# A first strip of 576 tokens, batch 1 normalised by token, and another order of loads, in a fused attention and bilinear feed-forward kernel

## The chip, the cores and the metric

One core of a Trainium2 chip runs the whole program. The metric is the device time in microseconds (us) of one execution; the time before is the median of three runs. The profile is one further execution of the same program, read engine by engine: PE is the matrix engine, PEld its weight loads, DVE the vector engine, ACT the scalar engine, POOL the GpSimd engine, SP the sync engine, which here issues stores and transposing DMAs.

## The reference

```python
kv  = einsum('bhsd,bhse->bhde', k, v)            # per batch b and head h, 64 x 64
x   = einsum('bhsd,bhde->bhse', q, kv)
x   = x / sqrt(mean(x * x, -1) + 1e-6) * g_norm  # RMS norm over the 64 of a head
x   = x.transpose(0, 2, 1, 3).reshape(4608, 512) # tokens by features
out = (x @ w_a) * (x @ w_b) @ w_out              # 512 -> 1536 -> 512
```

There are 8 batches of 576 tokens and 8 heads of 64. All inputs and the output are float32; the kernel multiplies in bfloat16 and accumulates in float32.

## The kernel before

The feed-forward part is cut into 9 strips of 512 tokens. `xt` holds x in bfloat16 with features on partitions, 4 blocks of 128. For a strip s, `ffn_ab(s, fc)` (line 389) computes one of 12 chunks of 128 hidden features: 4 matmuls with `wa_t` into one PSUM bank, a copy of it to SBUF by ACT (`part_a`), 4 matmuls with `wb_t` into another bank, and the product of both by DVE into `abt` (`part_b`). Then `ffn_o(s, g)` (line 434) computes the output of 128 tokens, g = 0 to 3, by 12 matmuls; `o_out` copies the bank to SBUF, on DVE when its running number is even and on ACT when it is odd, and `store` sends it out by SP in two pieces or so.

x comes from the attention of a batch, which is worked in between the matmuls of a strip. Strips do not end with batches: strip 2 is tokens 1024 to 1535, and batch 2 is tokens 1152 to 1727.

- Batch 0, at the start, and batch 1, between the output pieces of strip 0 (the loop over `pieces`, line 575), go **by feature**. For each of 4 pairs of heads: `qtr` transposes q on PE (12 matmuls), `kv1` makes k'v (12 matmuls), `x` or `px` multiplies, `psq` squares on ACT, `pss` sums the squares with a matmul against `ones` and takes the root on ACT, and `pst` scales on DVE straight into `xt`.
- Batches 2 to 7 go **by token**, in `slot(A, s, n)` (line 601), which is called after unit n of strip s, and with n - 0.5 in the middle of unit n. Units 0 to 11 are the chunks, 12 to 15 the output groups. `kv` makes k'v at `k0`; at `x0` `tx` makes x with tokens on partitions in 40 small matmuls, for 5 chunks c of 128 tokens (the last of 64). For each c then `tsq` squares (ACT), `tss` sums (DVE), `trs` takes the root (ACT) and multiplies it with g (POOL), and `txt` multiplies x with that (DVE) and has SP transpose the chunk into `xt` with a DMA.

Each engine runs its instructions in the order in which the code emits them, so the emission order is the schedule. POOL issues the loads and SP the stores and the transposing DMAs, each in that order too. Every POOL or SP DMA also waits for the one eight before it on its queue, whose semaphore it reuses.

`load_late(b)` (line 136) issues six DMAs on POOL for a batch from 2 on: two that rewrite q by token in bfloat16 into the DRAM tensor `qs`, and four that load k and v. For b > 2 it first has POOL copy one element of `qT[(b-1) % 2]`, so that it waits for the q of the batch before. `transpose_q(b)` (line 153) has SP transpose `qs` into `qT`. At the start POOL issues batch 0, then w_a and w_b in six chunks of 256 hidden features, then w_out in 12 pieces, batch 1 in 12 pieces, and `load_late(2)`.

`halves[0]` makes `product` issue two matmuls with 64 weight columns each in place of one with 128; such a pair runs side by side.

Of the kernel before, what the change touches and what calls it, by code (L numbers as in the profile page):

```python
# [15 lines left out]
def kernel(  # L16
# [11 lines left out]
    nc = tc.nc  # L28
# [14 lines left out]
    EARLY = 2  # L43
    KORD = tuple(range(KC))

    pool = ctx.enter_context(tc.tile_pool(name="sb", bufs=1))
    psum = ctx.enter_context(tc.tile_pool(name="ps", bufs=1, space=bass.MemoryType.PSUM))

# [17 lines left out]

    qT = [sb([128, NP, S], BF16, f"qT{i}") for i in range(2)]
    kvs = [sb([128, NP, D], BF16, f"kvs{i}") for i in range(2)]

    kvb = sb([128, NP, 128], BF16, "kvb")  # L70
    xt = sb([128, KC, n_tok], BF16, "xt")
    abt = [[sb([128, STRIP], BF16, f"ab{i}_{f}") for f in range(FC)] for i in range(2)]
    a_sb = [sb([128, STRIP], BF16, f"asb{i}") for i in range(4)]
    sq = [sb([128, 2, HF], BF16, f"sq{i}") for i in range(3)]
    rs = [sb([128, 2, HF], FP32, f"rs{i}") for i in range(3)]
# [58 lines left out]
        nc.gpsimd.dma_start(out=wo_t[:, i, :], in_=wo_v[:, i, :])  # L134

    def load_late(b):
        if b > EARLY:

            nc.gpsimd.tensor_copy(gate, qT[(b - 1) % 2][0:1, 0, 0:1])  # L139
        d = qs_d[b].rearrange("t (h d) -> t h d", h=H)  # L140
        for hs in (slice(0, NP), slice(NP, H)):
            nc.gpsimd.dma_start(out=d[:, hs, :], in_=q[b, hs].rearrange("h t d -> t h d"))  # L142
        n = 128 * LC
        for t, src in ((ktl[b % 2], k), (vtl[b % 2], v)):
            nc.gpsimd.dma_start(  # L145
                out=t[:, :, 0:LC, :],
                in_=src[b, :, 0:n].rearrange("h (t c) d -> t h c d", c=LC),
            )
            nc.gpsimd.dma_start(
                out=t[0 : S - n, :, LC, :], in_=src[b, :, n:].rearrange("h t d -> t h d")  # L150
            )
# [12 lines left out]
    class Attn:  # L164
# [5 lines left out]
        def kv(self, p, o):  # L170
# [5 lines left out]
            for c, n in enumerate(rows):  # L176
                for j in range(2):
# [4 lines left out]
                        start=(c == 0),  # L182
                        stop=(c == len(rows) - 1),
                    )

        def kv_out(self, ps, src):
            for j in range(2):
                r = slice(j * D, (j + 1) * D)
                nc.scalar.copy(kvb[r, ps, r], src[r])


        def kv1(self, p, i):
# [57 lines left out]
                )  # L250


        def x(self, p, i0):
            for h in range(2):
                product(
                    P[:, i0 + h, 0:HF],
                    kvb[:, p, :],
                    self.qT[:, p, h * HF : (h + 1) * HF],
                    start=True,
                    stop=True,  # L260
                )

        def rows(self, c):
            t0 = min(c * 128, S - 128)
# [19 lines left out]
        def tx(self, lent):  # L286
            self.lent = lent
            for c in range(LC + 1):
                t0, _ = self.rows(c)
                for p in range(NP):  # L290
                    for j, (i, c0) in enumerate(self.place(c)):
                        r = slice(j * D, (j + 1) * D)
                        nc.tensor.matmul(  # L293
                            P[:, i, c0 + p * D : c0 + (p + 1) * D],
                            lhsT=self.qT[r, p, t0 : t0 + 128],
                            rhs=self.kvs[r, p, :],
                            start=True,
                            stop=True,
                        )


            _, r = self.rows(LC)
            for j, (i, _) in enumerate(self.place(LC)):
                nc.scalar.copy(
                    x_last[r, j], P[r, i, 0 : STRIP // 2].rearrange("t (p d) -> t p d", p=NP)
                )

        def tsq(self, c):
            _, r = self.rows(c)
# [7 lines left out]
                axis=mybir.AxisListType.X,  # L317
            )

        def trs(self, c):  # L320
            _, r = self.rows(c)
            n = r.stop - r.start
            nc.scalar.activation(  # L323
                rst[c % 3][r],
                sst[c % 3][r],
                AF.Abs_reciprocal_sqrt,
                bias=eps_t[r],
                scale=1.0 / D,
            )
            nc.gpsimd.tensor_mul(  # L330
                sqt[c % 3][r].rearrange("t j p d -> t (j p) d"),
                rst[c % 3][r].unsqueeze(2).to_broadcast([n, H, D]),
                g_all[r].unsqueeze(1).to_broadcast([n, H, D]),
            )
# [13 lines left out]
    class Unit:  # L348
        n = 0

        def __init__(self, s, fc, a, b):
            self.s, self.fc, self.a, self.b = s, fc, P[:, a, :], P[:, b, :]
            self.t = a_sb[Unit.n % 4]
            Unit.n += 1

        def mm(self, w, kcs):
            t0 = self.s * STRIP
            for kc in kcs:
                product(
                    self.a if w is wa_t else self.b,  # L360
                    w[:, kc, self.fc * 128 : (self.fc + 1) * 128],
                    xt[:, kc, t0 : t0 + STRIP],
                    start=(kc == KORD[0]),
                    stop=(kc == KORD[-1]),
                )
# [2 lines left out]
            self.mm(wa_t, kcs)  # L368
            self.mm(wb_t, kcs)

        def part_a(self, kcs=KORD):
            self.mm(wa_t, kcs)
            nc.scalar.copy(self.t, self.a)  # L373

        def part_b(self, kcs=KORD):
            self.mm(wb_t, kcs)
            nc.vector.tensor_mul(abt[self.s % 2][self.fc], self.b, self.t)  # L377

        def rest(self, kcs=KORD):
            self.part_a(kcs)  # L380
            self.part_b(kcs)

    ab_banks = [4, 1, 2, 0]

# [4 lines left out]
    def ffn_ab(s, fc, between=None):  # L389
        u = Unit(s, fc, ab_bank(), 0)  # L390
        u.part_a()
        if between:
            between()
        u.b = P[:, ab_bank(), :]
        u.part_b()

    def store(t0, t, e0, e1, eng=nc.sync):
# [14 lines left out]
    n_o = [0]  # L412

    def o_mm(s, g, i, fcs, e0=0, e1=d_model):
        for fc in fcs:
            product(
                P[:, i, e0:e1],
                abt[s % 2][fc][:, g * 128 : (g + 1) * 128],
                wo_t[:, fc, e0:e1],
                start=(fc == 0),  # L420
                stop=(fc == FC - 1),
# [42 lines left out]
    make_identity(nc, ident, nomemset=True)  # L464
    nc.scalar.activation(warm, eps_t, AF.Abs_reciprocal_sqrt)
    nc.vector.memset(ones, 0.0)
    nc.vector.memset(kvb, 0.0)
    for t in ktl + vtl:
        nc.vector.memset(t[S - 128 * LC :, :, LC, :], 0.0)
    nc.vector.memset(ones[0:D, 0:D], 1.0 / D)  # L470
# [4 lines left out]
    for c in range(0, KC, 2):  # L475
        for w, src in ((wa_t, wa_v), (wb_t, wb_v)):
            nc.gpsimd.dma_start(out=w[:, c : c + 2, 0:WC], in_=src[:, c : c + 2, 0:WC])  # L477
    for i in range(1, d_ff // WC):
        load_ab(i * WC, (i + 1) * WC)
    for i in range(FC):  # L480
        load_o(i)
    for p in range(NP):
        load_pair(1, p)
    load_late(2)

    X, SS = (4, 0), 6

# [65 lines left out]
    u1.part_a((3,))  # L553
    u0.part_b((2, 3))
    u1.part_b((2, 3))

    u2 = Unit(0, 2, 0, 1)
    u3 = Unit(0, 3, 2, 0)
# [1 line left out]
    u3.part_a()  # L560
    u2.part_b()
    u3.part_b()
    for fc in range(4, FC):
        ffn_ab(0, fc)


    A = Attn(1)
    h1, h2 = range(0, FC // 2), range(FC // 2, FC)

    nc.sync.dma_start(out=gate_d, in_=vt[1][0:1, H - 1, EC - 1, D - 1 : D])  # L570
    nc.sync.dma_start(out=g_all, in_=g_norm.partition_broadcast(128))
    transpose_q(2)
    ffn_o(0, 0, X[0])
    pieces = [(1, h1), (1, h2), (2, h1), (2, h2), (3, h1), (3, h2)]
    for n, (g, fcs) in enumerate(pieces):

        halves[0] = n > 0
        o_mm(0, g, O, fcs)
        if fcs is h2:
            o_out(0, g, O)  # L580
        if 0 <= n - 2 < NP:
            A.pss(n - 2, SS)
            A.pst(n - 2, X[n % 2])
        if 0 <= n - 1 < NP:
            A.x(n - 1, X[(n - 1) % 2])
            A.psq(n - 1, X[(n - 1) % 2])
        if n < NP:
            A.qtr(n, 2)
            A.kv1(n, 2)
            A.kv_out(n, P[:, 2, STRIP - D :])  # L590
            A.qtr_out(n, 2)
    u0 = Unit(1, 0, 2, 3)
    u1 = Unit(1, 1, 4, 5)
    u0.first((0, 1, 2))
    u1.first((0, 1, 2))
    u0.rest((3,))
    u1.rest((3,))
    ab_banks[:] = [0, 1, 2]


    def slot(A, s, n):

        kb = P[:, 7, :].rearrange("q (b p e) -> q b p e", b=2, e=D)
        if s == 1:
            k0, xs = 5, (6.5, 8, 9.5, 11, 12.5)
        else:
            k0, x0 = {2: (2, 3.5), 3: (4, 5.5), 4: (0, 1.5), 5: (4, 5.5), 6: (0, 1.5)}[s]
            xs = tuple(x0 + x for x in (0, 1.5, 2.5, 4, 5))

        k0, x0 = {1: (5, 6.5), 2: (1, 2.5), 3: (4, 5.5), 4: (0, 0.5), 5: (4, 5.5), 6: (0, 0.5)}[s]  # L610
        if n == k0 and s in (1, 2, 3, 5):
            halves[0] = s < 5
            two = [A] if s < 3 else [A, Attn(s + 2)]
# [5 lines left out]
        m = n - x0  # L619
        if m == 0:  # L620
            A.tx(ab_bank())
        for c in range(LC + 1):
            if m == 1.5 * c:
                A.tsq(c)
            if m == (1, 2, 4, 5, 7)[c]:
                A.tss(c)
            if m == (1, 2, 4, 5, 7)[c] + 0.5:
                A.trs(c)
            if m == (1, 2, 4, 5, 7)[c] + 1.5:
                A.txt(c)  # L630

    for s in range(1, N_STRIP - 1):
        b = s + 1
        A = Attn(b) if b < B else None
        for n in range(FC + 4):
# [6 lines left out]
                slot(A, s, n)  # L642

            if s == 1 and n == 3:
                load_late(3)
            if b + 1 < B and n == (12, 4, 8, 5, 8)[s - 1]:
                transpose_q(b + 1)
            if b + 2 < B and n == (14, 10, 14, 8)[s - 1]:
                load_late(b + 2)
    last = N_STRIP - 1  # L650
    for fc in range(FC):
        ffn_ab(last, fc)
# [44 lines left out]
```

## Time and profile before

| | |
|---|---|
| time, median of 3 (lowest, highest) | 312.33 us (312.28, 312.47) |
| the profiled execution: time, span | 312.61 us, 310.8 us |
| granted PE clock | 1.00 of full speed |
| first matmul of strip 0 | about 13.9 us |
| last chunk of strip 0 begins | 33.43 us |
| first chunk of strip 1 begins | 49.96 us |
| first chunk of strip 2 begins | 82.75 us |
| matmul on the critical chain at | 60.69 to 307.8 us |
| loads: w_a, w_b all landed | 29.4 us |
| loads: w_out all landed | 37.3 us |
| loads: batch 1 all landed | 46.2 us |

The span runs from the first to the last instruction; the time of the execution has 1.8 us more around it. A row of the time-ordered view is: start, duration of the group, engine, source line, operation, output<-inputs, for matmuls the weight's rows and columns, then shape and count; in brackets, how long the engine was idle before and who released it. The durations of single matmuls overlap, since they are pipelined, so the step from start to start is what one costs. For the landing of a DMA the view of one line gives the time from issue to landing.

### The profile page before, as it was taken

The page shows a single profiled execution, that of the slowest core. Times are in us where ns is not written, and L with a number is a line of the kernel's source. Part 1 is how long each engine was busy: PE and PEld are TensorE (multiplying, and loading weights), DVE is VectorE, ACT ScalarE, POOL GpSimd, SP SyncE. Part 2 cuts the span into 40 slices and gives each one's busy share as a digit, 9 for nine tenths or more (in the row PEclk, how much of TensorE's full clock was granted, in tenths as well). Part 3 has the DMA queues.
Part 4 walks back from the last instruction along what each step waited for, and adds up shares of the span by engine and source line. Part 5 has one row for each costly group of instructions (what it writes and reads, how often), then busy time and mean ns, then how long its engine had stood idle before and what let it go on. Part 6 is the DMA issues. An engine that isn't in the chain of part 4 may idle for free.

```text
span 310.8 us, 6542 instructions
## 1 busy us (share of the span) xinstructions
PE 304.3 (98%) x2684; PEld 157.6 (51%) x2701; DVE 140.6 (45%) x235; ACT 117.0 (38%) x231; POOL 101.3 (33%) x123
## 2 busy tenths in 40 slices
PE   7899999999999999999999999999999999999996
PEld 3444476655555555555555555444444444444444
DVE  4544335458248603484386123752782143214321
ACT  3743255354255313551564034632651233123310
POOL 8954991093274630043646300221240000000000
PEclk9999999999999999999999999999999999999999
DMA  8999999999899999047998990073021200030002
GB/s 180 197 196 199 201 188 168 161 169 184 174 137 185 139 174 193 2 84 134 178 177 118 162 188 2 19 160 110 20 51 42 103 1 0 34 103 0 0 36 101
DMA packets 94403, 36.29 MB, mean 117 GB/s; under 512 B 64934, under 2 KB 89894, under 8 KB 94374
## 3 DMA queue, kind: packets, MB, share of 16 engines
q0 software_dynamic: 59120, 18.44, 56.6%
q1 hardware_dynamic: 34786, 16.93, 25.0%
q10 hardware_dynamic: 468, 0.51, 0.6%
q8 instruction: 21, 0.34, 0.5%
q14 instruction: 8, 0.07, 0.1%
HBM read 37.78 MB, written 12.98 MB: 163 GB/s over the span
## 4 chain that ended last, share of the span: by engine, by line
PE 79%; DMA 12%; POOL 7%; issue 1%; ACT 0%; POOLq 0%
PE P L161 77%; DMA wb_t<-in_moe_w_b_dram 6%; DMA vtl<-in_v_dram 4%; DMA wo_t<-in_moe_w_out_dram 2%; PE P L293 1%; PE P L178 1%; POOL vt L119 1%; POOL qt L119 1%; POOL qs L142 1%; POOL kt L119 1%; POOL wa_t L477 0%; POOL wb_t L477 0%; POOL wo_t L134 0%; POOL ktl L145 0%; POOL vtl L145 0%
## 5 line engine op out<-in xcount | busy, mean ns | idle before, releaser
L377 DVE TENSOR_TENSOR ab<-P,asb 128x512 bf16<-128x512 f32 x108 | 74.4, 691 | 103.2 <-PE P L161 99.9
L161 PE MATMUL P<-xt,wb_t 128*64 128x512 bf16 (+1 forms) x641 | 111.4, 379 | 0.2
L161 PE MATMUL P<-xt,wa_t 128*64 128x512 bf16 (+1 forms) x636 | 111.0, 379 | 0.6 <-issue 0.2
L373 ACT CAST asb<-P 128x512 bf16<-128x512 f32 x108 | 63.1, 586 | 89.6 <-PE P L161 89.5
L161 PE MATMUL P<-wo_t,ab 128*64 128x512 bf16 (+3 forms) x673 | 95.5, 371 | 0.3
L161 PEld LDWEIGHTS <-ab 128*64 128x64 bf16 (+1 forms) x678 | 47.5, 106 | 45.0
L161 PEld LDWEIGHTS <-wa_t 128*64 128x64 bf16 (+1 forms) x644 | 46.0, 106 | 46.2 <-issue 0.6
L161 PEld LDWEIGHTS <-wb_t 128*64 128x64 bf16 (+1 forms) x644 | 45.8, 106 | 45.8
L330 POOL TENSOR_TENSOR sqt<-rst,g_all 128x512 f32<-128x512 f32 (+1 forms) x24 | 25.0, 1046 | 83.0 <-ACT rst L323 83.0
L429 ACT COPY osb<-P 128x512 f32<-128x512 f32 x17 | 10.0, 586 | 70.2 <-PE P L161 60.2
L431 DVE COPY osb<-P 128x512 f32<-128x512 f32 x18 | 12.4, 691 | 44.9 <-PE P L161 40.4
L142 POOL DMA_DIRECT2D qs<-in_q_dram x12 | 19.8, 1654 | 0.7 <-issue 0.3
L314 DVE TENSOR_REDUCE sst<-sqt 128x8 f32<-128x512 f32 (+1 forms) x24 | 16.3, 680 | 1.7 <-ACT sqt L310 1.5
L339 DVE TENSOR_TENSOR qv<-P,sqt 128x512 bf16<-128x512 f32 x18 | 12.3, 681 | 0.0
L330 POOL TENSOR_TENSOR k_x<-rst,g_all 128x512 f32<-128x512 f32 x6 | 6.3, 1044 | 17.4 <-ACT rst L323 17.4
L323 ACT ACTIVATE rst<-sst,eps_t 128x8 f32<-128x8 f32 (+1 forms) x30 | 9.0, 300 | 7.2 <-DVE sst L314 7.0
L310 ACT ACTIVATE sqt<-P 128x512 f32<-128x512 f32 x18 | 10.5, 585 | 0.1
L243 DVE SCALAR_TENSOR_TENSOR xt<-P,g_col,rs 128x288 bf16<-128x288 f32 x16 | 7.5, 511 | 5.1 <-ACT rs L233 5.1
L134 POOL DMA_DIRECT2D wo_t<-in_moe_w_out_dram x12 | 6.4, 530 | 6.7 <-DMA wb_t<-in_moe_w_b_dram 3.2
L233 ACT ACTIVATE rs<-P,eps_t 128x576 f32<-128x576 f32 (+1 forms) x9 | 6.1, 689 | 3.7 <-PE P L161 3.4
L139 POOL COPY gate<-qT 1x1 bf16<-1x1 bf16 x5 | 0.9, 177 | 18.9 <-DVE kvs L618 14.0
L444 PE MATMUL P<-zeros 128*128 128x512 bf16 x16 | 5.8, 510 | 1.2 <-DVE eps_t L461 1.2
(72 smaller groups left out, 131.7 us busy)
## 6 DMA issues: line engine op xcount, KB each, us to landing
out_dram<-osb SPq DMA_DIRECT2D x23, 256.0 KB, 2.1
qs<-in_q_dram POOLq DMA_DIRECT2D x12, 288.0 KB, 7.5
ktl<-in_k_dram POOLq DMA_DIRECT2D x6, 512.0 KB, 9.6
vtl<-in_v_dram POOLq DMA_DIRECT2D x6, 512.0 KB, 12.2
out_dram<-osb SPq DMA_DIRECT2D x13, 128.0 KB, 2.4
wo_t<-in_moe_w_out_dram POOLq DMA_DIRECT2D x12, 128.0 KB, 6.0
wa_t<-in_moe_w_a_dram POOLq DMA_DIRECT2D x5, 256.0 KB, 8.9
wb_t<-in_moe_w_b_dram POOLq DMA_DIRECT2D x5, 256.0 KB, 9.5
```

The lines of the kernel that those rows point to most:

```text
L119: nc.gpsimd.dma_start(out=t[:, hs, :, :], in_=src[b, hs].rearrange("h (t c) d -> t h c d", c=EC))
L142: nc.gpsimd.dma_start(out=d[:, hs, :], in_=q[b, hs].rearrange("h t d -> t h d"))
L161: nc.tensor.matmul(o[r], lhsT=lhsT[:, r], rhs=rhs, **kw)
L310: nc.scalar.activation(sqt[c % 3][r], self.by_head(c)[r], AF.Square)
L314: nc.vector.reduce_sum(sst[c % 3][r], sqt[c % 3][r].rearrange("t j p d -> t (j p) d"), axis=mybir.AxisListType.X,)
L323: nc.scalar.activation(rst[c % 3][r], sst[c % 3][r], AF.Abs_reciprocal_sqrt, bias=eps_t[r], scale=1.0 / D,)
L330: nc.gpsimd.tensor_mul(sqt[c % 3][r].rearrange("t j p d -> t (j p) d"), rst[c % 3][r].unsqueeze(2).to_broadcast([n, H, D]), g_all[r].unsqu ...
L339: nc.vector.tensor_mul(t[r].rearrange("t (p j) d -> t j p d", j=2), self.by_head(c)[r], sqt[c % 3][r])
L373: nc.scalar.copy(self.t, self.a)
L377: nc.vector.tensor_mul(abt[self.s % 2][self.fc], self.b, self.t)
L429: nc.scalar.copy(t, P[:, i, :])
L431: nc.vector.tensor_copy(t, P[:, i, :])
```

## The change

- **Strip 0** keeps 512 tokens in its output groups, but its chunks now cover all 576 tokens of batch 0: each unit has 448 columns, and `ffn_end` does columns 448 to 575 for two chunks at a time, in 16 matmuls of 128 columns with one ACT copy and two DVE products. Strip 1 then has 448 columns, 576 to 1023. `abt` becomes one tile of 1024 columns per chunk.
- **Batch 1** goes by token: `qtr` and `kv1` of its pairs stand after chunks 5, 8, 10 and 11 of strip 0, `tx` after the last chunk, and the ACT, DVE and POOL steps are written out, with one product with g on DVE. The four output groups of strip 0 follow. `x`, `kv_out`, `kvb` and its memset go.
- **Loads.** The pieces of batch 1 are issued among the chunks of w_a and w_b, ahead of w_out. For batch 2 the k and v loads come before those of q, later than before; `g_all` is loaded early.
- **Strip 1** starts its first two units in two column parts (256 and 192). Its `slot` makes k'v at n = 8 and x at n = 9, in place of 5 and 6.5, with its own offsets; the last 64 tokens of batch 2 are sent during strip 2. `transpose_q(2)` moves to unit 3 of strip 1, and `load_late(4)` from unit 14 of strip 1 to unit 3 of strip 2.

```diff
-    abt = [[sb([128, STRIP], BF16, f"ab{i}_{f}") for f in range(FC)] for i in range(2)]
+    abt = [sb([128, 2 * STRIP], BF16, f"ab{f}") for f in range(FC)]
...
+    def ffn_end(fc, i):
+        n = S - CUT
+        t = a_sb[Unit.n % 4][:, 0 : 2 * n]
+        Unit.n += 1
+        for m, w in enumerate((wa_t, wb_t)):
+            for j in range(2):
+                for kc in KORD:
+                    product(
+                        P[:, i, (2 * m + j) * n : (2 * m + j + 1) * n],
+                        w[:, kc, (fc + j) * 128 : (fc + j + 1) * 128],
+                        xt[:, kc, CUT:S],
...
+        nc.scalar.copy(t, P[:, i, 0 : 2 * n])
+        for j in range(2):
+            nc.vector.tensor_mul(
...
-    for i in range(1, d_ff // WC):
-        load_ab(i * WC, (i + 1) * WC)
+    load_ab(WC, 2 * WC)
+    load_ab(2 * WC, 3 * WC)
+    load_pair(1, 0)
+    load_ab(3 * WC, 4 * WC)
+    hs = [slice(2 * p, 2 * p + 2) for p in range(NP)]
+    load_heads(1, qt[1], q, hs[1])
+    load_heads(1, kt[1], k, hs[1])
+    load_ab(4 * WC, 5 * WC)
+    load_heads(1, vt[1], v, hs[1])
+    load_heads(1, qt[1], q, hs[2])
+    load_ab(5 * WC, 6 * WC)
+    load_heads(1, kt[1], k, hs[2])
+    load_heads(1, vt[1], v, hs[2])
+    load_pair(1, 3)
     for i in range(FC):
         load_o(i)
-    for p in range(NP):
-        load_pair(1, p)
-    load_late(2)
...
     for fc in range(4, FC):
+        if fc == 9:
+            ab_banks.remove(4)
         ffn_ab(0, fc)
+        if fc in (5, 8, 10, 11):
+            halves[0] = True
+            pair((5, 8, 10, 11).index(fc))
+        if fc % 2:
+            ffn_end(fc - 1, (ab_banks[0] if fc == FC - 1 else 6 + fc // 2 % 2))
+    lent = ab_banks[1]
+    A.tx(lent)
+    A.tsq(0)
+    A.last_out(0)
+    A.tsq(1)
+    A.tss(0)
+    A.trs(0)
+    A.tsq(2)
+    A.tss(1)
+    A.trs(1)
+    A.last_out(1)
+    A.tss(2)
+    A.txt(0)
+    A.trs(2)
+    A.tsq(3)
+    A.txt(1)
+    A.tss(3)
+    A.trsqrt(3)
+    A.txt(2)
+    A.tg(3, nc.vector)
+    A.txt(3)
+    A.tsq(4)
+    A.tss(4)
+    A.trsqrt(4)
+    load_late_kv(2)
+    A.tg(4, nc.gpsimd)
+    load_late_q(2)
+    three = (ab_banks[2], ab_banks[0], ab_banks[1])
+    for fc in range(FC + 2):
+        for g, i in enumerate(three):
+            f = fc - (0, 0, 2)[g]
+            if 0 <= f < FC:
+                o_mm(0, g, i, (f,))
+                if f == FC - 1:
+                    o_out(0, g, i)
+    ffn_o(0, 3)
+    u0 = Unit(1, 0, 4, 5)
+    u1 = Unit(1, 1, 6, 7)
+    c = 256
+    for u in (u0, u1):
+        u.mm(wa_t, KORD, (0, c))
+        u.mm(wb_t, KORD, (0, c))
+    for u in (u0, u1):
+        u.part_a(KORD, (c, u.n))
+        u.part_b(KORD, (c, u.n))
+    A.txt(4)
...
-        k0, x0 = {1: (5, 6.5), 2: (1, 2.5), 3: (4, 5.5), 4: (0, 0.5), 5: (4, 5.5), 6: (0, 0.5)}[s]
+        k0, x0 = {1: (8, 9), 2: (1, 2.5), 3: (4, 5.5), 4: (0, 0.5), 5: (4, 5.5), 6: (0, 0.5)}[s]
...
+        if s == 1:
+            sqs, sums = (0, 1.5, 3, 4, 5), (1, 2, 3.5, 5, 6)
+            rss, outs = (1.5, 2.5, 4, 5.5, 6), (2.5, 3.5, 5, 6, 8)
+        else:
+            sqs, sums = (0, 1.5, 3, 4.5, 6), (1, 2, 4, 5, 7)
+            rss, outs = (1.5, 2.5, 4.5, 5.5, 7.5), (2.5, 3.5, 5.5, 6.5, 8.5)
...
             if s == 1 and n == 3:
+                transpose_q(2)
                 load_late(3)
+            if s == 2 and n == 0:
+                Attn(2).txt(LC)
             if b + 1 < B and n == (12, 4, 8, 5, 8)[s - 1]:
                 transpose_q(b + 1)
-            if b + 2 < B and n == (14, 10, 14, 8)[s - 1]:
+            if b + 2 < B and n == (None, 10, 14, 8)[s - 1]:
                 load_late(b + 2)
+            if s == 2 and n == 3:
+                load_late(4)
```

## The prediction

> **What bounds the kernel now.** I read the page first, then the waits, then the time-ordered view of PE, of DVE and of SP.
>
> ```profile
> span 310.8 us, 6542 instructions
> ...
> PE 304.3 (98%) x2684; PEld 157.6 (51%) x2701; DVE 140.6 (45%) x235; ACT 117.0 (38%) x231; POOL 101.3 (33%) x123
> ```
>
> PE is busy 98%. Busy PE need not be PE at its peak, so I compare with the step from matmul to matmul.
>
> ```profile
> 21.34 1.03 PE L161 MATMUL P<-xt,wa_t 128*128 128x512 bf16 x4
> ...
> 34.29 1.03 PE L161 MATMUL P<-xt,wb_t 128*128 128x512 bf16 x4
> 35.15 4.05 PE L161 MATMUL P<-wo_t,ab 128*128 128x512 bf16 x17
> ...
> 43.31 0.44 PE L161 MATMUL P<-sq,ones 128*64 128x288 bf16 x4
> 43.55 0.44 PE L161 MATMUL P<-qT,kvb 128*64 128x288 bf16 x4
> 43.80 0.45 PE L202 MATMUL P<-ident,qt 96*64 96x96 bf16 x12
> 44.05 0.38 PE L178 MATMUL P<-vt,kt 96*64 96x64 bf16 x12
> 44.24 1.49 PE L161 MATMUL P<-wo_t,ab 128*64 128x512 bf16 x12
> ...
> 49.96 0.84 PE L161 MATMUL P<-xt,wa_t 128*64 128x512 bf16 x6
> ```
>
> From 21.34 to 34.29 lie 15 groups of 4: 12.95 / 60 = **0.2158 us** per matmul of 512 columns, without a hole. Four half matmuls of 288 columns take 43.55 - 43.31 = 0.245, so 0.1225 per pair. Two points give 0.0025 us + 0.4165 ns per column: 448 columns 0.189, 256 0.109, 192 0.083, 128 0.056. From 14 us to 308 us this step repeats; the largest waits of PE after the start are single ones of 0.3:
>
> ```profile
> PE P L161 <- ACT sq L225: 0.3, 1, 0.3
> ...
> PE P L178 <- DMA vt<-in_v_dram: 0.3, 1, 0.3
> ```
>
> So PE is the bound. An edit counts only as far as it takes matmul steps out, or makes PE wait.
>
> **What the Trainium skill says.** "TensorE: Matmul & The Clock Gate", section "Wait — 56ns, not 53.3ns?": a warm matmul costs its columns at 2.4 GHz plus about 2.5 ns; the trace agrees (0.2158 at 512 columns). "TensorEngine Tiling (Array Packing)", "Key Properties": a change of tiling mode drains the engine; here the 40 matmuls of `tx` last 0.69 but PE resumes 0.81 after the step before. "DMA: Bandwidth & Descriptors", "Queues, rings and completion order": each DMA engine takes turns between queues by packet. In this trace an SP transpose fares worse than turns suggest: issued at 70.61, behind six POOL loads of batch 3, it landed 7.2 later; from 200 us on, with none, 2.3 to 2.5.
>
> **PE work.** Between 35.15 and 49.96 PE spends 14.81, of which 48 output matmuls are 10.36. The other 4.45 is batch 1: `x` 4 x 0.245 = 0.98, `pss` 0.98, four times `qtr` and `kv1` at 0.44 = 1.76, and 0.73 of switches and waits for batch 1's loads. After it: `qtr` and `kv1` still 1.76; `x`, `pss` and the 0.73 go (**-2.69**); one `tx` comes (**+0.81**). Columns in all are unchanged (448 + 128 + 448 = 1024), but there are 96 matmuls more in `ffn_end` and 16 more in the split units: 112 x 2.5 ns = **+0.28**. Steps of half matmuls at 128 columns are not in the trace; weight loads need not bind, since half matmuls of 64 columns with new weights each go at 1.26 us for 80. Bounds: 0 to +0.3. Net **-1.6**, so strip 2 could start at 82.75 - 1.6 = 81.15.
>
> **Loads of the first strip.** POOL's queue delivers a piece of batch 1 each 0.74 and a 256-column half chunk each 1.34. In the new order w chunks 3, 4 and 5 come 3, 5 and 7 pieces later: the last at 29.4 + 5.2 = 34.6, w_out from 38.9 to 46.2. A pair of chunks now takes 16 x 0.189 + 16 x 0.056 = 3.92 (before 3.45), with 0.44 per head pair; chunk 10 needs its w_b at about 36, the output groups need w_out from 40.7, three matmuls (0.65) per piece, as fast as pieces land (0.65). Slack 1.4 or more: cost 0. If the rate fell by 5%, the slack would go.
>
> **Batch 1's chain.** `tx` ends near 40.6. By the rows 0.585 (square), 0.68 (sum), 0.30 (root), 1.05 (POOL product), 0.68 (DVE product) the chunks leave DVE at about 44.0, 44.9, 46.3 and 47.8. The product with g on DVE is not in the trace; I take 0.69, between 0.68 (DVE, same size from PSUM) and POOL's 1.05. The 48 output matmuls (10.36) and the first column part (16 x 0.109 = 1.75) cover this until 52.7, when PE needs chunks 2 and 3. The transposes themselves take 2.4 free. But the k and v loads of batch 2 go out from POOL at about 45.2, ahead of the last two, and need 8 us from 46.2: the last transpose lands between 50.2 and 54. Cost 0 to 1.3; I take **+0.4**. ACT's and DVE's work for strip 0 fits: per pair of chunks some 1.5 and 1.9 of 3.9.
>
> **Batch 2's loads and q.** k and v land by 54.5, q (4.2 before) by 58.5; `transpose_q(2)` takes 4.6 when nothing else runs, so qT is there at 63, for `tx` at 67: cost 0, slack 4. SP stands at that transpose from about 56; nothing behind it is due before 73. `load_late(3)` follows on POOL at 63.5 (before 62.4); its six issues take 6.4 there, so `tg(0)` of batch 2 can run from 70, when it is due. Its loads end at 80 (before 78.9).
>
> **Where PE will wait.** Strip 2 needs chunk 2 of batch 2 (tokens 1408 to 1535). Its `txt(2)` had m = 5.5 after 6.5, unit 12; now m = 5 after 9, **unit 14**, emitted behind `o_out(1, 2)`. How long that takes after an output group is in the trace, at unit 12:
>
> ```profile
> 75.19 0.69 DVE L431 COPY osb<-P 128x512 f32<-128x512 f32 x1 [0.83 <-PE P L161]
> 75.80 0.68 DVE L339 TENSOR_TENSOR qv<-P,k_x 128x512 bf16<-128x512 f32 x1
> ```
>
> ```profile
> 75.91 1.11 SPq L409 DMA_DIRECT2D out_dram<-osb  x2
> 77.11 2.58 SPq L343 DMA_TRANSPOSE xt<-qv  x1
> 79.86 2.55 SPq L154 DMA_TRANSPOSE qT<-qs  x1
> ```
>
> The group ended at 75.0; copy, product and the two stores on SP bring the transpose out 2.1 later, and it needs 2.4 more: 4.5. Before, three groups (7.8) covered that. Now one does: 12 x 0.2158 = 2.59. PE waits at least 4.5 - 2.6 = **2.0** at the head of strip 2. This cannot be less unless DVE or SP get there earlier.
>
> It can be more, on SP's queue. `transpose_q(3)` stood behind `txt(2)`; now it stands ahead of `txt(1)`, both stores of groups 1 and 2 and `txt(2)`. It starts at about 75.5, while the loads of batch 3 run until 80. Free it holds SP 2.5; among loads it held SP 7.1 at 50.54. I let it go at 78.3; then `txt(1)` 1.2, two stores 1.1, two more 1.1: the transpose goes out at 81.4 in place of 80.7, +0.6. At the other end, 7.1, it goes out near 86: +5. Cost of this wait **+2.6**, bounds 2.0 and 7.
>
> From strip 2 on loads, slots and stores keep their places relative to PE; `load_late(4)` waits on POOL for qT of batch 3 as before (84.5), so its later place costs 0. The memset of `kvb` (0.27 on DVE, while it waits for the first q) and the early load of `g_all` are off the path: 0.
>
> **Sum.** -1.6 + 0.4 + 2.6 = +1.4. The profiled execution, 312.61 with 1.8 around the span, would become 314.0; the median of the runs is 0.28 lower: **313.7**.
>
> **Rivals.**
> 1. Only the bare wait: SP free in time, batch 1 in time. -1.6 + 2.0 = +0.4: 312.7. For it: the loads of batch 3 may be done by then. It is within 0.2%, about what a measurement here can tell from no change.
> 2. No wait, so faster. Chunk 2 is in place when strip 2 begins, and the 1.6 of PE work is all that is seen: 310.7. It decides at one point: the transpose has to land within 2.6 of the end of unit 14. For it speaks that DVE is busy only 45% of the time, against it the emission order and the 4.5 measured above.
> 3. SP held long by `transpose_q(3)`, as at 50.54: wait 5 to 7; 312.33 - 1.6 + 0.4 + 5.5 = 316.6. A wait over 3.4 may also lower PE's clock for a while ("TensorE: Matmul & The Clock Gate", Part 1); the first dummy matmuls, at about 0.43 each, show what that costs.
>
> **Numbers.** Forecast 0.52 (own range 312.95 to 315.2), rival 1 0.20, rival 2 0.13, rival 3 0.15. Faster 0.13, same 0.20, slower 0.67. The range takes in rival 1, the slower part of rival 2 (some of the 1.6 lost) and half of rival 3: 311.6 to 316.5.
>
> **What would show it.** In the profile after: no `x`, no `ones` matmul after 16 us; strip 1's second unit pair near 54; a PE idle of 2 to 3 before the first `wa_t` matmul of strip 2, released by the transpose into `xt`; on SP `transpose_q(3)` before it, lasting over 2.5; perhaps a hole near 53. I am wrong if strip 2 begins without a hole, if PE waits for w_a, w_b or w_out in strip 0, or if 128-column steps exceed 0.056.

## The result and the profile after

The changed kernel takes **327.59 us** (327.23 to 327.94, 4 runs) against 312.38 us (312.28 to 312.47, 4 runs) for the kernel before: ratio 1.0487, 95% interval 1.0469 to 1.0505. It is 15 us slower, not 1.4. Two executions of the versions below, one of 323.94 us and one of 357, ran at a lower clock than the others of their kernel and are left out of the times given.

The page of the changed kernel: span, busy time of the engines, and PE's busy share and granted clock in 40 slices of 8.1 us.

```profile
span 325.5 us, 7136 instructions
...
PE 307.1 (94%) x2967; PEld 162.3 (50%) x2967; DVE 145.8 (45%) x249; ACT 117.7 (36%) x237; POOL 105.5 (32%) x127
...
PE   7999996999539999999999999999999999999996
...
PEclk9999999999958999999999999999999999999999
```

PE is no longer full in three slices, the 7th and the 11th and 12th, and its clock is low in the 12th and 13th. After that the row looks like the one of before: the loss lies ahead of 106 us. The view of waits names it (engine, line, releaser: us in all, times, longest):

```profile
POOL gate L139 <- DMA qT<-qs: 17.3, 3, 15.5
...
PE P L167 <- DMA xt<-qv: 12.2, 3, 8.9
```

The kernel before had no wait of PE over 0.3 behind the start. Now PE waits three times for a transposing DMA into `xt`, and POOL waits 15.5 once for the transposed q. PE's time-ordered view gives the places:

```profile
41.26 10.70 PE L167 MATMUL P<-wo_t,ab 128*64 128x512 bf16 x96
53.48 0.63 PE L167 MATMUL P<-xt,wa_t 128*64 128x256 bf16 x8 [1.52 <-DMA xt<-qv]
...
57.23 0.52 PE L167 MATMUL P<-xt,wa_t 128*64 128x192 bf16 x8 [1.81 <-DMA xt<-qv]
...
75.15 10.53 PE L167 MATMUL P<-wo_t,ab 128*64 128x512 bf16 x96
94.54 1.92 PE L167 MATMUL P<-xt,wa_t 128*64 128x512 bf16 x8 [8.86 <-DMA xt<-qv]
```

From matmul to matmul the gaps are 51.59 to 53.48, 55.15 to 57.23 and 85.30 to 94.54: two small ones in strip 1's first units, and 9.2 us at the head of strip 2. A gap, here and below, is counted from start to start, so it contains one ordinary step of 0.1 to 0.2. SP's view shows what stood ahead of that last transpose (start, us for which SP was held, operation):

```profile
44.93 5.61 SPq L341 DMA_TRANSPOSE xt<-qv  x4
50.63 6.89 SPq L430 DMA_DIRECT2D out_dram<-osb  x8
...
65.74 2.48 SPq L160 DMA_TRANSPOSE qT<-qs  x1
78.92 1.24 SPq L341 DMA_TRANSPOSE xt<-qv  x1
80.24 1.21 SPq L430 DMA_DIRECT2D out_dram<-osb  x2
81.62 6.62 SPq L160 DMA_TRANSPOSE qT<-qs  x1
88.33 1.22 SPq L341 DMA_TRANSPOSE xt<-qv  x1
89.64 1.94 SPq L430 DMA_DIRECT2D out_dram<-osb  x4
91.68 1.20 SPq L341 DMA_TRANSPOSE xt<-qv  x1
```

`transpose_q(3)` (81.62) holds SP for 6.62 while the loads of batch 3 run until 89.4; chunk 1, four stores and chunk 2 (91.68) follow in order. The shape is the one that the prediction described; each item is 7 to 10 us later than it said. Last, strip 2 starts slowly. The windows view, with the granted clock in the column after POOL's:

```profile
94.50:101.00 6.50, 6.46 (x55) 3.41 (x57) 1.45 (x3) 1.17 (x2) 3.53 (x5) 0.58 1.87 165
101.00:110.00 9.00, 9.00 (x143) 5.17 (x138) 4.93 (x9) 4.56 (x10) 1.76 (x2) 1.00 1.51 170
```

The 32 half matmuls from 94.54 take 6.11 (the next one starts at 100.65), where 16 steps of 0.2158 are 3.45: 2.7 more.

### The profile page after: what moved, and what is told of

The parts are those of the page before. It is cut to its first block, busy times and chain, and to the rows that moved or that the text cites. A ratio compares the mean times of both kernels' runs of the same rounds, so it can differ in the third digit from the quotient of the medians.

```text
span 325.5 us, 7136 instructions
## 1 busy us (share of the span) xinstructions
PE 307.1 (94%) x2967; PEld 162.3 (50%) x2967; DVE 145.8 (45%) x249; ACT 117.7 (36%) x237; POOL 105.5 (32%) x127
## 4 chain that ended last, share of the span: by engine, by line
PE 89%; DMA 5%; SPq 2%; DVE 2%; ACT 1%; issue 1%; POOL 0%; DVEq 0%
PE P L167 84%; DMA xt<-qv 3%; PE P L184 1%; PE P L283 1%; DMA qv<-in_q_dram 1%; SPq L160 1%; PE P L203 1%; DVE qv L337 1%; ACT sqt L301 1%; SPq L430 1%; PE P L217 0%; PE P L466 0%; ACT sq L226 0%; SPq L341 0%; POOL sqt L328 0%
## 5 line engine op out<-in xcount | busy, mean ns | idle before, releaser
L167 PE MATMUL P<-xt,wa_t 128*64 128x512 bf16 (+7 forms) x764 | 114.8, 357 | 12.4 <-DMA xt<-qv 12.2
L379 DVE TENSOR_TENSOR ab<-P,asb 128x512 bf16<-128x512 f32 (+1 forms) x108 | 72.9, 676 | 114.8 <-PE P L167 102.9
L167 PE MATMUL P<-xt,wb_t 128*64 128x512 bf16 (+7 forms) x764 | 113.8, 355 | 0.0
L375 ACT CAST asb<-P 128x512 bf16<-128x512 f32 (+1 forms) x108 | 61.9, 574 | 96.0 <-PE P L167 95.8
L167 PEld LDWEIGHTS <-wa_t 128*64 128x64 bf16 (+1 forms) x764 | 49.4, 108 | 56.9 <-issue 13.3
L167 PEld LDWEIGHTS <-wb_t 128*64 128x64 bf16 (+1 forms) x764 | 49.9, 108 | 44.0 <-issue 1.5
L328 POOL TENSOR_TENSOR sqt<-rst,g_all 128x512 f32<-128x512 f32 (+1 forms) x27 | 28.1, 1044 | 93.6 <-ACT rst L317 93.6
L305 DVE TENSOR_REDUCE sst<-sqt 128x8 f32<-128x512 f32 (+1 forms) x28 | 19.1, 680 | 2.1 <-ACT sqt L301 1.9
L283 PEld LDWEIGHTS <-qT 64*128 64x128 bf16 x280 | 4.5, 95 | 2.5 <-issue 2.4
L120 POOL DMA_DIRECT2D qt<-in_q_dram x7 | 4.7, 670 | 3.0 <-DMA wa_t<-in_moe_w_a_dram 1.1
```

The costliest lines, as they stand in the source:

```text
L167: nc.tensor.matmul(o[r], lhsT=lhsT[:, r], rhs=rhs, **kw)
L283: nc.tensor.matmul(P[:, i, c0 + p * D : c0 + (p + 1) * D], lhsT=self.qT[r, p, t0 : t0 + 128], rhs=self.kvs[r, p, :], start=True, stop=True,)
L305: nc.vector.reduce_sum(sst[c % 3][r], sqt[c % 3][r].rearrange("t j p d -> t (j p) d"), axis=mybir.AxisListType.X,)
L328: eng.tensor_mul(sqt[c % 3][r].rearrange("t j p d -> t (j p) d"), rst[c % 3][r].unsqueeze(2).to_broadcast([n, H, D]), g_all[r].unsqueeze(1 ...
L379: nc.vector.tensor_mul(abt[self.fc][:, self.c0 : self.c0 + self.n], self.b, self.t)
```

## The experiments

The theory after the result was: the hole at strip 2 is the end of one chain through two queues (batch 2's loads on POOL, `transpose_q(2)` on SP, batch 3's loads on POOL, `transpose_q(3)` and chunk 2 on SP), and SP's transposes and stores, mixed with the loads, stretch it. The rivals were that the late emission of chunk 2 alone makes the hole, and that the order of k, v and q does. Each edit is shown by its main lines; `...` stands for lines that are not shown.

**Parts alone, in the kernel before.** First the order of batch 2's loads (`EARLY` is 2):

```diff
+        if b > EARLY:
+            load_late_q(b)
+            load_late_kv(b)
+        else:
+            load_late_kv(b)
+            load_late_q(b)
```

> Kernel before, with batch 2's k and v issued ahead of its q, this part of the change alone. Theory: qT of batch 2 lands 2 to 4 us later than 61.8, PE waits for it in unit 7 of strip 1 (0 to 2 us), batch 3's loads end 2 to 4 us later, near 82, and strip 2 waits 0 to 1.5; time 312.5 to 315. Rival (order harmless): 312.4.

Measured: 312.53 us (12 runs), ratio 1.0003 (0.9994 to 1.0011). No difference. qT landed at 61.0, no later than the 61.8 of before; the expectation had missed that. The reason is in the loads: here SP has hardly any work among them, and all six took from 41.0 (first issue) to 56.3 (last landing), 15.3. In the kernel before, with `transpose_q(2)` among them, it was 41.3 to 60.6, 19.3.

To it come the steps of strip 1, in two versions: q transposed at its old place on SP, or behind strip 0's stores. ("The same" in the first expectation means the second version.)

```diff
-        k0, x0 = {1: (5, 6.5), ...
+        k0, x0 = {1: (8, 9), ...
...
+        if s == 1:
+            sqs, sums = (0, 1.5, 3, 4, 5), (1, 2, 3.5, 5, 6)
+            rss, outs = (1.5, 2.5, 4, 5.5, 6), (2.5, 3.5, 5, 6, 8)
...
+            if s == 2 and n == 0:
+                Attn(2).txt(LC)
...
+            if s == 2 and n == 3:
+                load_late(4)
```

> The same with transpose_q(2) back ahead of strip 0's stores, so that q of batch 2 is as early as before: the late emission of chunk 2 in unit 14 and transpose_q(3) ahead of it are left. My blind price for the late emission was 2.0 (4.5 from the end of the group to landing, less one group of 2.59). Theory: qT lands at 61, batch 3's loads end near 79 and hold neither; hole 2.0 to 2.8 at strip 2; time 314.3 to 315.3. Rival (transpose_q(3) holds SP among the loads all the same): hole 4 to 7, 316.5 to 320.

Measured: 318.58 us, ratio 1.0191 (1.0178 to 1.0204), within the rival's range. SP's view and PE's view of this run:

```profile
74.32 1.22 SPq L353 DMA_TRANSPOSE xt<-qv  x1
75.65 1.16 SPq L419 DMA_DIRECT2D out_dram<-osb  x2
76.98 3.73 SPq L164 DMA_TRANSPOSE qT<-qs  x1
80.80 1.22 SPq L353 DMA_TRANSPOSE xt<-qv  x1
82.11 1.96 SPq L419 DMA_DIRECT2D out_dram<-osb  x4
84.16 1.19 SPq L353 DMA_TRANSPOSE xt<-qv  x1
```

```profile
86.81 1.92 PE L171 MATMUL P<-xt,wa_t 128*64 128x512 bf16 x8 [4.15 <-DMA xt<-qv]
```

Here qT landed at 61.3 and batch 3's loads at 78.5, about as early as the prediction assumed. `transpose_q(3)` still holds SP 3.73, and the gap at strip 2 is 4.5 (82.28 to 86.81), then about 2.4 us are lost to the clock, which is at half until 91.6. Against the 312.62 of the kernel before on the same chip, strip 1's new steps, with the order of loads that costs nothing by itself, cost 6.0 us.

```diff
-    transpose_q(2)
...
             if s == 1 and n == 3:
+                transpose_q(2)
                 load_late(3)
```

> Kernel before (strips of 512, batch 1 by feature) with the change's timing of strip 1 alone: batch 2's k and v ahead of q, transpose_q(2) at unit 3 behind strip 0's stores, k'v at 8 and x at 9 with the change's steps, last chunk of batch 2 in strip 2, load_late(4) at unit 3 of strip 2. Theory (the root of the changed kernel's 9 us hole is that q of batch 2 lands at 70.4, and that comes from batch 1's four transposes meeting the loads): here qT lands at 61 to 65, batch 3's loads end at 78 to 82, a hole of 2 to 5 at strip 2; time 314.5 to 318. Rival (the timing of strip 1 makes the hole by itself): 9 us and a slow clock, 323 or more. Rival (nothing of it matters without the first strip's change): 312.4.

Measured: 320.68 us, ratio 1.0249 (1.0217 to 1.0281). qT landed at 65.0, batch 3's loads at 83.1, `transpose_q(3)` held SP 6.06, the gap is 6.9: between the theory's 2 to 5 and the rival's 9, and the time 2.7 above the theory's range. q 3.7 later made the hole 2.4 longer, as the chain says. But the root that the theory named, batch 1's four transposes, isn't needed: no transpose of batch 1 exists here. The six loads took 18.9 (41.3 to 60.15) with the eight stores of strip 0 among them, and 15.3 (41.3 to 56.6) in the version before, from which this one differs only in the place of `transpose_q(2)`. This pair is the cleanest evidence that SP's work stretches the loads.

**The order on the queues, in the changed kernel.**

```diff
+    nc.gpsimd.tensor_copy(gate, x_tok[1][0:1, 0, 0, 0:1])
     load_late_kv(2)
```

> Changed kernel, with batch 2's loads held on POOL until the fourth product of batch 1 has left DVE (one 1x1 copy on POOL that reads it). Theory (transposing DMAs land behind the POOL loads that were issued before them): the transposes of chunks 1 to 3 land 2.5 to 3 us after issue in place of 7 to 8, and the two holes of PE ahead of strip 1 (1.9 and 2.0 us) fall to under 0.5. The hole at strip 2 is set by the loads and SP, which do not move earlier, so it grows by about as much: time 326 to 328.5, no gain. Rival (each hole is a cost of its own): the same fall of the first holes, strip 2's hole stays at 9, time 323 to 324. Rival (the transposes are slow by themselves): first holes stay, 327.6.

Measured: 331.69 us, ratio 1.0613 (1.0591 to 1.0634): slower still, and above the range of the theory and of both rivals. Chunks 1 and 2 of batch 1, which now met no load, landed in 2.4 to 2.5, and the first hole went. Chunk 3, issued at the same moment as the first load, took 6.8, and a gap of 2.5 stayed. The loads, now beside one transpose, the eight stores of strip 0 and later chunk 4, still took 19.3 (48.85 to 68.17), and all of it 2.6 to 2.7 later: PE waited 3.1 for qT in strip 1, and the gap at strip 2 grew to 11.3.

```diff
-            if b + 1 < B and n == (12, 4, 8, 5, 8)[s - 1]:
+            if b + 1 < B and n == (14, 4, 8, 5, 8)[s - 1]:
```

> Changed kernel, with transpose_q(3) moved on SP from unit 12 of strip 1 to unit 14, behind the transpose of chunk 2 of batch 2. Theory (SP's order and the loads of batch 3 both hold that chunk): it goes out at 85 in place of 91.7, and lands when batch 3's loads end, 89.5 to 91; the hole falls from 9 to 4 to 6 us and time to 322 to 324.5. Rival A (only the late emission counts, as I priced it: 4.5 us after the group): strip 2 begins at 87.5, hole 2.0, time 317 to 319. Rival B (the loads alone hold it, SP's order is harmless): no gain, 327.6.

Measured: 322.09 us (318.87, 322.09 and 322.98), ratio 1.0289 (1.0227 to 1.0351), as expected, though the fastest of the three lies in rival A's range. With `transpose_q(3)` behind chunk 2, about 5 of the 15 us are back.

```diff
+    load_late_q(2)
     load_late_kv(2)
     A.tg(4, nc.gpsimd)
-    load_late_q(2)
```

> Changed kernel, with batch 2's q issued ahead of its k and v, and both ahead of the last product with g on POOL. Theory (the hole at strip 2 starts with q landing late: qT of batch 2 at 70.4, only then the loads of batch 3, until 89.4): qT lands near 66, the loads of batch 3 end near 85, strip 2 begins near 90; time 322 to 325. The holes ahead of strip 1 stay within 1 us of 3.9. Rival (the order of q and of k, v is harmless): 327.6.

Measured: 323.94 us, ratio 1.036 (1.0324 to 1.0397): the time was as expected, the reason only in part. qT landed at 68.8, 1.6 earlier, not 4; one early hole of 2.8 was left, and strip 2 began at 95.0, not near 90. In that execution, the slowest of the four, chunk 2's transpose came to lie among the loads of batch 4 and took 5.3.

```diff
-    load_late_kv(2)
     A.tg(4, nc.gpsimd)
+    load_late_kv(2)
     load_late_q(2)
+    transpose_q(2)
...
             if s == 1 and n == 3:
-                transpose_q(2)
```

> Changed kernel, with batch 2's loads behind the last product with g on POOL (so that they start after batch 1's four transposes have landed), and transpose_q(2) on SP ahead of strip 0's stores (so that the stores come after the loads). Theory (transposes and stores of SP and the loads of POOL hold each other up when they run together): the six loads take 11 to 13 us in place of 18.8, qT of batch 2 lands at 66 to 69 in place of 70.4 although they start 5 later, both holes ahead of strip 1 fall under 0.5, strip 2 begins at 89 to 92 in place of 94.5; time 321 to 325. Rival (the loads take their time by themselves): they last 18, qT lands at 75, time 329 to 333, as in the run that only held k and v back.

Measured: 326.39 us, ratio 1.0452 (1.0425 to 1.048), above the range expected. The view of the transposes' line between 44 and 58 us, of the changed kernel and of this one:

```profile
DMA to landing us min/median/max: 2.5/7.1/8.1
```

```profile
DMA to landing us min/median/max: 2.4/2.5/2.6
```

Kept apart from the loads, all four transposes land in 2.4 to 2.6, and both early holes are gone. Yet PE's view shows:

```profile
70.36 0.76 PE L283 MATMUL P<-kvs,qT 64*128 64x64 bf16 x40 [2.68 <-DMA qT<-qs]
...
94.17 1.92 PE L167 MATMUL P<-xt,wa_t 128*64 128x512 bf16 x8 [7.89 <-DMA xt<-qv]
```

The loads, with nothing of SP among them, took 14.7 in place of 19.5, but began 4.8 later (50.9 for 46.1), and qT landed at 70.3, as in the changed kernel (70.4). So PE reaches that point earlier, waits there, and strip 2 begins 0.4 earlier than in the changed kernel. The early holes were no separate cost: without them PE only waits longer for the chain.

The move of `transpose_q(3)` once more, on top of the version before:

```diff
-            if b + 1 < B and n == (12, 4, 8, 5, 8)[s - 1]:
+            if b + 1 < B and n == (14, 4, 8, 5, 8)[s - 1]:
```

> The kernel of the run before with transpose_q(3) on SP at unit 14, behind the transpose of chunk 2. Theory: that chunk goes out 2 us after the third output group of strip 1 (81 to 82) and lands near the end of batch 3's loads, 85 to 88; hole 3 to 6; time 317 to 321. Rival (only the late emission counts): hole 2.0, 312.5 to 313.5.

Measured: 323.34 us, ratio 1.0342 (1.0328 to 1.0356). The gap at strip 2 fell from 8.3 to 5.9, within what was expected; the time missed its range by 2.3. Chunk 2 was issued at 85.8, where 81 to 82 was expected, and PE could go on at 91.9, just after batch 3's loads were done (91.2).

**Can the schedule be mended?** The four versions below build on that kernel with the loads and transposes apart, each on the one before.

```diff
-        k0, x0 = {1: (8, 9), 2: (1, 2.5), ...
+        k0, x0 = {1: (8, 9.5), 2: (4, 5), ...
...
+            sqs, sums = (0, 0.5, 1.5, 3, 4.5), (0.5, 1.5, 2, 3.5, 5.5)
+            rss, outs = (1, 2, 2.5, 4, 5.5), (2, 2.5, 3, 5, 8)
...
+                if s == 1 and c == 2:
+                    transpose_q(3)
...
-                load_late(3)
+                nc.gpsimd.tensor_copy(gate, qT[0][0:1, 0, 0:1])
+                load_late_q(3)
+            if s == 1 and n == 14:
+                load_late_kv(3)
```

> The same two moves, and: batch 2's x at unit 9.5 of strip 1 with closer steps, so that its chunk 2 goes out in the middle of unit 13, transpose_q(3) right behind it; of batch 3 only q is loaded before that, k and v after unit 14, its k'v and x come at units 4 and 5 of strip 2 in place of 1 and 2.5; load_late(5) at unit 11 in place of 10. Theory (PE work is 1.5 less, all the rest was waits on transposes): no hole ahead of strip 1, under 1.5 at strip 2, PE clock full; time 310.8 to 312.6, at or below the kernel before. Rival (the first strip of 576 tokens costs more on PE than it saves): 313 or more without holes.

Measured: 325.73 us, ratio 1.04 (1.0377 to 1.0424). A miss of 13 us. The hole at strip 2 is gone, but three others came: 2.1 for qT of batch 2, 5.3 for k and v of batch 3, 3.6 for those of batch 5, and a half clock after two of them.

```diff
-    load_late_kv(2)
     load_late_q(2)
+    load_late_kv(2)
...
-        k0, x0 = {1: (8, 9.5), 2: (4, 5), ...
+        k0, x0 = {1: (9, 9.5), 2: (7, 8), ...
...
-                if s == 1 and c == 2:
-                    transpose_q(3)
+                if s < 3 and c == 2:
+                    transpose_q(s + 2)
...
-            if b + 2 < B and n == (None, 11, 14, 8)[s - 1]:
+            if b + 2 < B and n == (None, 14, 14, 8)[s - 1]:
```

> The retuned kernel, with q of batch 2 ahead of its k and v again (still behind batch 1's transposes), k'v of batch 2 at unit 9, of batch 3 at unit 7 and x at unit 8 of strip 2 with closer steps, transpose_q(4) behind chunk 2 of batch 3, load_late(5) at unit 14, and k'v of batch 5 in strip 4 by itself in place of with batch 4's. Theory: the waits that the retuned kernel got in exchange (2.1 for qT of batch 2, 5.3 for k and v of batch 3, 3.6 for batch 5, and the slow clock after them) fall away or to under 1 each, PE work is 1.5 less: 310.8 to 313. Rival (each load that is moved meets another transpose or store): 315 or more.

Measured: 313.72 us (15 runs, 312.32 to 316.96), ratio 1.0043 (1.0022 to 1.0065): just above the range expected. Its page:

```profile
span 310.9 us, 7129 instructions
...
PE   7999999999999999999999999999999999999995
...
PEclk9999999999999999999999999999999999999999
```

No hole over 0.75 is left and the clock is full, 14 us better than the change. But the profiled execution, one of the faster, only has the span of the kernel before (310.8), and the median of the runs is 1.1 above that of the kernel before on the same chip (312.62). In the profiled execution the saved 1.6 went into a start of strip 0 0.3 later, 0.26 at the first output matmuls, and 0.47 and 0.45 for v of batches 2 and 3: 1.5 in all.

```diff
-        k0, x0 = {1: (9, 9.5), 2: (7, 8), ...
+        k0, x0 = {1: (9.5, 10), 2: (8, 8.5), ...
...
-            rss, outs = (1, 2, 2.5, 4, 6), (2, 2.5, 3, 5, 7)
+            rss, outs = (1, 2, 2.5, 4, 6), (2, 2.5, 3, 5, 6.5)
```

> The retuned version with q first, with the two k'v products that PE waited for put half a unit and one unit later (k0 and x0 of strip 1: 9.5 and 10, of strip 2: 8 and 8.5), and the later steps of the chain closer together. In the version before, PE waited 0.47 and 0.45 us for the v of batches 2 and 3, 0.26 at the first output matmuls and 0.3 at the start, which together ate the 1.6 us of PE work that the change removes. Theory (the waits are all that is between this and the work saved): both v waits go, 311.8 to 312.4 us, at best 0.2% under the kernel before. Rival (the chain is now so close that what is moved later makes the next thing late: chunk 2 lands within 1.6 us of strip 2's start): 312.8 to 314.5, with a new wait at the head of strip 2 or 3.

Measured: 321.64 us, ratio 1.0298 (1.0282 to 1.0313). The waits for v went, as the theory said; the price came at the head of strip 2 (a gap of 1.1) and of strip 3 (5.8), and was larger than the rival's. POOL's view, then PE's:

```profile
114.83 0.18 POOL L139 COPY gate<-qT 1x1 bf16<-1x1 bf16 x1 [4.00 <-DMA qT<-qs]
115.07 3.30 POOL L146 DMA_DIRECT2D qs<-in_q_dram  x2
...
121.59 1.03 POOL L328 TENSOR_TENSOR sqt<-rst,g_all 64x512 f32<-64x512 f32 x1
```

```profile
124.13 1.92 PE L167 MATMUL P<-xt,wa_t 128*64 128x512 bf16 x8 [5.46 <-DVE ab L379]
```

Half a unit had moved the last product with g behind the loads of batch 5. POOL waits there for qT and issues six DMAs, 10.8 us in all (from 110.83); DVE stands at the product with x that needs it, the products `ab` of strip 3 stand behind that on DVE, and PE waits for them.

```diff
-        k0, x0 = {1: (9.5, 10), 2: (8, 8.5), ...
+        k0, x0 = {1: (9, 9.5), 2: (8, 8.5), ...
...
-            if b + 2 < B and n == (None, 14, 14, 8)[s - 1]:
+            if b + 2 < B and n == (None, 15, 14, 8)[s - 1]:
```

> The version before left strip 1's steps half a unit later, so that chunk 2 landed 0.04 us ahead of its use and PE waited 1.13 us at strip 2; and POOL's product with g of batch 3's last chunk came to stand behind the six loads of batch 5, which cost 5.8 us at strip 3. Here strip 1 is as in the retuned version with q first (wait of 0.47 for v of batch 2), k'v and x of batch 3 stay at 8 and 8.5, and batch 5's loads go out one unit later, behind that product. Theory: no wait is left but 0.47, 0.26 and 0.3: 311.8 to 312.6 us, the saved PE work less these, 0 to 0.2% under the kernel before. Rival: the shorter chain of batch 3, half a unit later, is late again in strip 3, or the later loads of batch 5 are: 313 to 316.

Measured: 313.36 us (14 runs, 312.01 to 314.34), ratio 1.0016 (1.0002 to 1.003): above the range expected, and in the rival's, but for neither of its reasons. The hole at strip 3 is gone; in the profiled execution PE waits 1.5 for qT of batch 2 instead. Up to there this kernel is the version of 313.72, where PE did not wait at that place, which suggests that this wait comes and goes from execution to execution. Both versions spread over 2.3 us or more, while the kernel before stays within about 1; that fits chains without slack, but it isn't shown. No version here beat the kernel before.

## Why the prediction was wrong, step by step

- **PE work -1.6: right within 0.3.** From strip 0's first matmul to strip 2's first PE had 68.87 before (13.88 to 82.75). Now it has 80.27 (14.27 to 94.54), less 12.7 for the three gaps (13.2, of which 0.5 are ordinary steps): 67.6, so -1.3. In the version of 313.72 it is 68.02 (14.19 to 82.21) less waits of 0.73: 67.3, so -1.6. The 128-column steps cost 0.056, as worked out: 8 pairs in 0.45 (26.48 to 26.93).
- **Loads of the first strip, cost 0: right.** The last w_b landed at 35.2 (34.6 predicted), w_out from 39.5 to 46.8; PE waited for neither.
- **Batch 1's chain, +0.4 with bounds 0 and 1.3: wrong size, 3.7.** The chunks left DVE within 1.5 of the working. Issued at 46.35, 47.65 and 49.06, three transposes took 7.0, 7.3 and 8.1, so that the last landed at 57.2, where I had it by 54 at the latest. That the loads do it is shown by the apart version: 2.4 to 2.6 without loads beside them.
- **Batch 2's loads and q, "cost 0, slack 4": the step that failed.** "k and v land by 54.5, q by 58.5" took 13.3 from the first issue at 45.2, put together from parts. The issue came 0.9 later and the loads took 19.5. With SP quiet these six loads take 13.9 to 15.3 (five runs), with its transposes or stores among them 18.9 to 21.0 (five runs); and the trace of before had the whole of it, 19.3 with a transpose among them. I charged the transposes for the loads, but not the loads for SP's work, and I measured q's lateness only against its use by `tx`, though q's landing also sets when batch 3's loads go out.
- **"Where PE will wait", +2.6 with bounds 2.0 and 7: mechanism right, size 9.** The lateness went down the chain, in us:

| event | predicted | measured | late |
|---|---|---|---|
| q of batch 2 landed | 58.5 | 65.6 | 7.1 |
| qT of batch 2 landed | 63 | 70.4 | 7.4 |
| loads of batch 3 landed | 80 | 89.4 | 9.4 |
| SP released by `transpose_q(3)` | 78.3 | 88.2 | 9.9 |
| chunk 2's transpose issued | 81.4 | 91.7 | 10.3 |

PE came later too, at 85.5 in place of 81.55 (the early holes, above all), so the hole grew by 6.4 and not by 10. Even with q early (the version of 318.58) the gap was 4.5, not the 2.6 that I chose: there `transpose_q(3)` held SP 3.73, to 80.7. "I let it go at 78.3" was too kind by itself; the lateness did the rest.
- **Rival 3's clock: right, and left out of the sum.** "TensorE: Matmul & The Clock Gate", Part 1, of the Trainium skill gives half rate after an idle window of about 3.4 us, and windows that run freely; here the gap of 9.2 was followed by a clock of 0.58 over 6.5 us, +2.7. It belonged into the sum of every case with a hole, since gaps from 2.5 on could bring it here (last section).
- **Sum.** -1.3 + 0.4 (strip 0 starts later) + 3.7 + 9.0 (the gap less a step) + 2.7 = 14.5; the spans differ by 14.7 (325.5 - 310.8). The sum says where PE's time went, not what each item would give back: the apart version removed the 3.7, and strip 2 began only 0.4 earlier.

How much of this is the change's own? Strip 1's new steps make 6.0 (318.58), q behind the stores 2.1 more (320.68). The other 7 come with the new first strip. Three things there can make them: batch 2's loads go out at 46.1 and not at 41.3, since batch 1's chain stands before them on POOL; transposes lie among them; and strip 1's units are shorter (448 columns for 512), so PE is sooner at what the chain delivers. The apart version, which took the second away and made the first worse, came out 1.2 faster, with intervals that overlap, so no gain is shown; no run separates the three further. Nor does any run have the late emission of chunk 2 by itself, with q early and `transpose_q(3)` behind that chunk: whether it costs the 2.0 that I priced stays open. "DMA: Bandwidth & Descriptors", section "Queues, rings and completion order", of the Trainium skill has each DMA engine take turns between queues by packet, and has the signal that a DMA of SP is complete wait for every earlier write of that DMA engine, whatever its queue. By the turns alone a transpose would pass quickly, and 7 to 8 us against 2.5 doesn't agree. The wait fits in part: chunks 1 and 2 of batch 1 landed 0.3 and 0.9 after the k loads issued just ahead of them (53.03 and 54.01), but chunk 3 landed at 57.19, ahead of both v loads issued before it (58.93 and 60.96). For the loads there is a plainer reading that no run tests: by the DMA view the eight stores move 1.0 MB beside the 1.7 MB of the six loads, so they may just share the DMA engines. Why loads and SP's DMAs hold each other up so long stays open.

## What to carry to other kernels

Follow a late transfer through every queue that it releases, to the end: here a load 7 us late released a queue that released loads that held another queue, and PE paid only there, 30 us on. Price a DMA by how it runs beside those that will be in flight with it, in both directions. Removing a hole ahead of such a chain's end returned almost nothing here (0.4 of 3.7), since the chain set the next one; check what it is waiting for before counting the gain.

## What the runs showed of the hardware

- A transposing DMA issued in the same moment as a load from POOL landed after 6.8 us, the two just ahead of it after 2.4 to 2.5.
- The six loads of batch 2 took 13.9 to 15.3 us with SP quiet and 18.9 to 21.0 with its transposes or stores among them, also where it was one transpose of 128 tokens and the stores (19.3). With q first and one transpose of q midway, as in the last three versions, they took 16.4 to 16.7.
- Over all runs an SP transpose of q held its queue 2.0 to 3.6 us when no load issued before it was in flight, and 5.2 to 8.6 when three or four were.
- Gaps of PE of 2.5, 2.7 and 3.04 us were each followed by about 3.4 us at half clock (three of the runs above); others of 2.8 and 3.06 were not. The traces show what decides. Behind the start, half clock always lasts 3.41, 6.83 or 10.24 us: the clock changes only on a grid of steps of 3.41 us, which lies differently in each execution. A step at full clock in which PE was busy for 1.34 us or less was followed by half clock, in each of 15 cases; no step with 1.44 or more was. From half clock PE came back after a step with 2.9 busy or more, and not after one with 2.5 or less. For example, the gap of 2.7 (the version of 323.34) left 1.06 busy in the step from 67.98 to 71.39, and the next was at half clock; the gap of 3.06 (the version of 331.69) lay across two steps, with 1.9 and 2.2 busy, and cost no clock. (The end of a matmul is modelled in these traces, so the limit is good to a tenth or so.)
